# An attention and two feed-forward blocks on one core: more subtractions and the landmark sums issued to GpSimd

## The chip, the core and the metric

The kernel runs on one core of one Trainium2 chip. A core has five engines with a queue of instructions each, which they work off in order: TensorE (PE; its weight loads are PEld), VectorE (DVE), ScalarE (ACT), GpSimd (POOL) and SyncE (SP), which here issues every DMA. The metric is device time in microseconds (us), the median of three runs.

## The reference, cut to what matters

```python
def _attn_ref(q, k, v):                       # 4 batches, 8 heads, 576 positions, 64 wide
    q_lm = q.reshape(B, H, 32, S // 32, D).mean(axis=3)   # 32 landmarks: means of 18 positions
    k_lm = k.reshape(B, H, 32, S // 32, D).mean(axis=3)
    A, Bm, C = sm(q, k_lm), sm(q_lm, k_lm), sm(q_lm, k)   # three softmaxes
    Z = Bm.T / (norm_1(Bm) * norm_inf(Bm) + 1e-06)        # then 6 times: Z = 2 Z - Z Bm Z
    return A @ Z @ C @ v

def reference(...):
    x = attention as 2304 tokens x 512
    h = x @ w_in;   y = (h * cos(h)) @ w_out              # 512 -> 2048 -> 512
    h2 = y @ w_in2; return prelu(h2, alpha) @ w_out2      # 512 -> 2048 -> 512
```

All data are float32. q and k are drawn eight times as large as v.

## The kernel before, in words

**Split numbers.** A product of float32 matrices is made of three TensorE products. Each operand is held as a high half (a rounding copy, made by ScalarE) and a low half (the operand minus the high half, made by a subtraction). The subtractions all go through the helper `sub` at L323, so in the profile they are `L323 TENSOR_TENSOR`, on VectorE (DVE) or on GpSimd (POOL). `split` makes both halves of a tile 512 or 576 wide; `hl` does it for the second block's weights, `y_load` for its input (256 wide), and `tick` and `btick` for the activations (288 and 512 wide).

**First stage, some 535 us.** Attention runs in units of two batches and two heads: four units at the start (`unit`, m = 0) and four more later (m = 1), each group followed by the iteration for Z (`z_path`). `vprime` folds attention's last factor into the first weight matrix. The first block then runs as 128 ticks (`tick`): one tick is a product of 6 matmuls into a PSUM bank `h` (L986), the chain ACT L991, DVE L993, ACT L995 and L996, DVE L997 that makes h cos(h), its high half (ACT L1000), its low half (L323, 288 wide), and 12 matmuls of the second product (L1013). There are two banks `h`; L997 is the last reader of a bank, so L986 of the tick after next waits for it. The second four units, and `convert`, which turns the 64 pieces of weights from 64-bit to 32-bit numbers in three VectorE instructions (L474, L476, L478) with a DMA ahead and often one behind, run between the ticks.

**Landmark sums.** A landmark is a sum over 18 positions. Nine of these lie along the free axis of a tile, and that part is one VectorE reduction over 1152 elements: L609 for six of the eight sums of the first units, L645 for the eight of the second units. The other two of the first units go through nine matmuls each (L620), a copy and a transpose.

**Second stage, some 380 us.** The second block takes 512 tokens at a time; one `btick` is seven products of 256 columns (L1257, one level of Strassen's scheme), their combination on VectorE (L1280), the activation (L1321, L1324), its halves (L1326, L323) and 24 matmuls of 512 columns (L1338). A last piece of 256 tokens uses L1302.

**What sets the order.** The class `Plan` takes every operation with its dependencies, a duration for each engine that may do it, and a due time, and lays them out engine by engine on a model of time; what it puts out is the fixed order of each engine's queue. Where an operation may go to two engines, it is given to the one that ends it first by that model, after a bias is taken off: 0.2 us for POOL and for ACT (`PB`, `AB`). The tiles share memory areas with a fixed number of buffers per name (three of `cf`, which `convert` uses, three of `raw`). An operation can be placed once the buffer it needs has been given up. In the profile, and in the rows of order below, nearly all SBUF tiles read `m`; `h`, `x` and `acc` are PSUM banks.

## Time and profile before

| | before |
|---|---|
| time, median of three runs | 916.64 us |
| lowest of the runs | 913.74 us |
| the profiled execution, its own time | 916.43 us |
| its span, from first to last instruction | 914.6 us |
| TensorE busy, granted clock (mean) | 835.4 us, 0.958 |
| VectorE busy | 680.6 us |
| ScalarE busy | 501.1 us |
| GpSimd busy | 181.8 us |

Busy time is a sum over the whole span. The two stages have different limits, so the shares have to be read stage by stage. The granted clock is a share of 2.4 GHz. A row's duration on VectorE or GpSimd runs from start to end of the instruction and includes any time in which it stands still.

### The profile page before, as it was taken

The numbers are of one execution on the slowest core, as the hardware profiler recorded it, in microseconds if no ns is written. First come the engines' busy times: TensorE is split into PE (matmuls) and PEld (weight loads), VectorE is DVE, ScalarE is ACT, GpSimd is POOL, SyncE is SP. The second block draws the span as 40 slices with busy tenths as digits, with TensorE's granted clock in tenths as the row PEclk, the third lists the DMA queues.
The fourth block names the chain that finished last, engine by engine and source line by source line (L and its number), as shares of the span: only waits on it lengthen the run. The fifth ranks groups of instructions, "written<-read, shape, count | busy, mean of one in ns | idle before, by whom it ended". The sixth has DMA issues, their size and how long they took to land.

```text
span 914.6 us, 15709 instructions
## 1 busy us (share of the span) xinstructions
PE 835.4 (91%) x5674; PEld 749.3 (82%) x5674; DVE 680.6 (74%) x1316; ACT 501.1 (55%) x1165; POOL 181.8 (20%) x182
## 2 busy tenths in 40 slices
PE   5885889896999899999898989999999999999997
PEld 4563778684888889899888978999999899998896
DVE  6889978889898677988998686875566556556663
ACT  4754769687667576575766843353344234433431
POOL 2022231212113011312542222310021012000100
PEclk8895899797999999999999999999999999999999
DMA  9978699978769899798557421113013111310140
GB/s 229 238 225 238 193 239 206 229 166 246 207 191 286 271 310 304 232 309 303 165 184 239 135 84 47 47 58 82 24 47 99 52 35 57 83 35 25 48 126 23
DMA packets 98013, 144.42 MB, mean 158 GB/s; under 512 B 28560, under 2 KB 63888, under 8 KB 97936
## 3 DMA queue, kind: packets, MB, share of 16 engines
q1 hardware_dynamic: 97936, 143.43, 54.0%
q8 instruction: 44, 0.72, 0.3%
q14 instruction: 33, 0.27, 0.1%
HBM read 96.35 MB, written 38.67 MB: 148 GB/s over the span
## 4 chain that ended last, share of the span: by engine, by line
PE 54%; DVE 20%; DMA 15%; ACT 5%; issue 4%; SPq 1%; POOL 0%; DVEq 0%; ACTq 0%; POOLq 0%
PE acc L1338 21%; PE h L1257 9%; PE x L1257 7%; PE acc L1013 6%; DMA m<-in_moe_w_out_dram 3%; PE h L986 3%; DVE m L323 3%; DMA m<-w1d 2%; DVE m L476 2%; DVE m L478 2%; DVE m L997 2%; DVE m L993 2%; DMA y1d<-m 1%; DMA m<-in_moe_w_in_dram 1%; DVE m L474 1%
## 5 line engine op out<-in xcount | busy, mean ns | idle before, releaser
L323 POOL TENSOR_TENSOR m<-m,m 128x288 fp32r<-128x288 f32 (+4 forms) x149 | 151.2, 1021 | 559.3 <-ACT m L1000 201.6
L1013 PE MATMUL acc<-m,m 128*128 128x288 f32 x1536 | 239.5, 304 | 3.3 <-DVE m L1033 2.4
L1013 PEld LDWEIGHTS acc<-m,m 128*128 128x128 f32 x1536 | 219.9, 194 | 8.9 <-issue 4.4
L1338 PE MATMUL acc<-m,m 128*128 128x512 f32 x864 | 208.4, 393 | 0.8 <-DVE m L323 0.4
L323 DVE TENSOR_TENSOR m<-m,m 128x512 fp32r<-128x512 f32 (+4 forms) x283 | 177.3, 648 | 41.5 <-ACT m L458 16.6
L1338 PEld LDWEIGHTS acc<-m,m 128*128 128x128 f32 x864 | 159.4, 189 | 32.4 <-DVE m L323 0.9
L986 PE MATMUL h<-m,m 128*128 128x288 f32 x768 | 132.5, 310 | 30.9 <-DVE m L997 25.1
L986 PEld LDWEIGHTS h<-m,m 128*128 128x128 f32 x768 | 113.0, 196 | 41.5 <-DVE m L997 32.9
L1257 PE MATMUL h<-m,m 128*128 128x256 f32 x768 | 106.3, 281 | 0.4 <-ACT m L318 0.4
L1326 ACT ACTIVATE m<-m 128x512 fp32r<-128x512 f32 (+1 forms) x80 | 46.3, 588 | 109.0 <-DVE m L1324 106.5
L1257 PEld LDWEIGHTS h<-m,m 128*128 128x128 f32 x768 | 99.2, 188 | 2.9 <-ACT m L318 0.6
L1280 DVE TENSOR_TENSOR m<-h,m 128x512 f32<-128x512 f32 x32 | 22.1, 690 | 81.9 <-ACT m L318 81.9
L1257 PE MATMUL x<-m,m 128*128 128x256 f32 x576 | 80.3, 283 | 1.8 <-ACT m L318 1.8
L1000 ACT ACTIVATE m<-m 128x288 fp32r<-128x288 f32 x128 | 55.9, 443 | 43.0 <-DVE m L997 40.8
L318 ACT ACTIVATE m<-h 128x256 f32<-128x256 f32 (+3 forms) x105 | 42.2, 404 | 64.3 <-PE h L1257 58.7
L1257 PEld LDWEIGHTS x<-m,m 128*128 128x128 f32 x576 | 73.0, 188 | 3.6 <-ACT m L318 2.0
L995 ACT ACTIVATE m<-m 128x288 f32<-128x288 f32 x128 | 56.0, 443 | 30.7 <-DVE m L993 30.2
L1117 ACT ACTIVATE m<-m 128x512 fp32r<-128x512 f32 x68 | 41.4, 628 | 43.7 <-PE h L1257 20.0
L997 DVE SCALAR_TENSOR_TENSOR m<-m,h 128x288 f32<-128x288 f32 x128 | 56.3, 446 | 10.1 <-ACT m L996 9.6
L993 DVE SCALAR_TENSOR_TENSOR m<-h,m 128x288 f32<-128x288 f32 x128 | 57.1, 448 | 8.2 <-ACT m L991 7.7
L991 ACT ACTIVATE m<-h 128x288 int32<-128x288 f32 x128 | 51.6, 403 | 20.4 <-PE h L986 19.9
L458 ACT ACTIVATE m<-m 128x512 fp32r<-128x512 f32 (+1 forms) x72 | 45.2, 631 | 28.3 <-DMA m<-w1d 18.5
(156 smaller groups left out, 949.6 us busy)
## 6 DMA issues: line engine op xcount, KB each, us to landing
m<-in_moe_w_out_dram SPq DMA_DIRECT2D x32, 512.0 KB, 5.2
m<-in_moe_w_in_dram SPq DMA_DIRECT2D x32, 512.0 KB, 5.6
m<-wi2d SPq DMA_DIRECT2D x56, 256.0 KB, 3.2
y1d<-m SPq DMA_DIRECT2D x40, 288.0 KB, 4.8
m<-w1d SPq DMA_DIRECT2D x32, 256.0 KB, 4.8
m<-m SPq DMA_DIRECT2D x32, 256.0 KB, 4.5
vvd<-m SPq DMA_DIRECT2D x32, 256.0 KB, 4.6
m<-vvd SPq DMA_DIRECT2D x16, 512.0 KB, 6.0
```

The source lines that it names most:

```text
L323: ENG[e].tensor_tensor(o, a, b, op=ALU.subtract)
L458: op(act(n), lambda e: nc.scalar.activation(hi.t[:, 0:n], sl(f.t), AF.Copy), r=[f], w=[hi, lo], target=target, after=after)
L986: nc.tensor.matmul(out=hp.t[:, 0:CW], lhsT=w_[:, js], rhs=x[:, cs], start=(i == 0), stop=(i == 5))
L991: op(act(CW, True), lambda e: nc.scalar.activation(k_.t, hp.t[:, 0:CW], AF.Copy, scale=INV2PI), r=[hp], w=[k_], target=T + 0.8)
L993: op(dve(CW), lambda e: nc.vector.scalar_tensor_tensor(u.t, hp.t[:, 0:CW], INV2PI, k_.t, op0=ALU.mult, op1=ALU.subtract), r=[hp, k_], w=[u])
L995: op(act(CW), lambda e: nc.scalar.activation(u.t, u.t, AF.Sin, scale=math.pi), rw=[u], aset="sin")
L997: op(dve(CW), lambda e: nc.vector.scalar_tensor_tensor(hc.t, u.t, 1.0, hp.t[:, 0:CW], op0=ALU.subtract, op1=ALU.mult, reverse0=True), r=[h ...
L1000: op(act(CW), lambda e: nc.scalar.activation(gh.t, hc.t, AF.Copy), r=[hc], w=[gh, gl])
L1013: nc.tensor.matmul(out=yg[o].t[:, 0:CW], lhsT=w_.t[:, sl], rhs=x.t, start=(j == ja and i == 0), stop=(j == jb and i == 2),)
L1257: nc.tensor.matmul(out=rv(k), lhsT=a_.t[:, p, c2, js], rhs=b_.t[:, q_, c2, 0:hw], start=(first and c2 == 0 and i == 0), stop=(c2 == 1 and ...
L1326: op(act(w), lambda e, m_=m_, gh=gh: nc.scalar.activation(gh.t[:, 0:w], m_.t[:, 0:w], AF.Copy), r=[m_], w=[gh, gl])
L1338: nc.tensor.matmul(out=ya[n][t].t, lhsT=gv(x_), rhs=r_.t, start=(st and k == 0), stop=(en and k == 2))
```

## The change

The plan's cost of an elementwise operation on GpSimd goes from n/480 + 0.15 us to n/440 + 0.3 us, and a new bias `SB` = 1.6 us takes the place of `PB` = 0.2 us for POOL, so that an operation that may go to VectorE or GpSimd goes to GpSimd unless it would end there over 1.6 us later by the model. The landmark sums of the first units may go to VectorE (one reduction, as before) or to GpSimd, where they are four additions of halves and a copy; the form with matmuls (L620) is gone. Those of the second units go to GpSimd always, as five additions, with a buffer of `cf` for the partial sums.

```diff
-KN = dict(..., PB=0.2, AB=0.2, ..., LM=126, ..., QN=2, KA=0.004, ...)
+KN = dict(..., PB=0.2, AB=0.2, ..., QN=2, SB=1.6, KA=0.004, ...)
+        def bias(o, x):
+            return KN["SB"] if x == "POOL" else BIAS.get(x, 0.0)
-                        max(free[x], o.est, sl) + dx - BIAS.get(x, 0.0) < s + d - BIAS.get(e, 0.0)
+                        max(free[x], o.est, sl) + dx - bias(o, x) < s + d - bias(o, e)
     def pool(n):
-        return ("POOL", n / 480.0 + 0.15)
+        return ("POOL", n / 440.0 + 0.3)
@@ landmark sums, first units (a: 128 x 1152)
-                    op(dve(1152), lambda e, a=a, ls=ls: nc.vector.tensor_reduce(...))       # L609
-                    ... or nine matmuls, a copy and a transpose                             # L620
+                    x = a.t.rearrange("p (h r d) -> p h r d", h=2, d=D)
+                    y = ls.t.rearrange("p (h r d) -> p h r d", h=2, d=D)
+                    add(y, x[:, :, 0:4], x[:, :, 4:8])
+                    add(y[:, :, 0:2], y[:, :, 0:2], y[:, :, 2:4])
+                    add(y[:, :, 0:1], y[:, :, 0:1], y[:, :, 1:2])
+                    z = ls.t[:, P:2 * P].rearrange("p (h d) -> p h d", h=2)
+                    add(z, y[:, :, 0], x[:, :, 8])
+                    nc.gpsimd.tensor_copy(ls.t[:, 0:P], ls.t[:, P:2 * P])
+                op([("POOL", 3.9), ("DVE", 2.1)], lm, r=[a], w=[ls])
@@ landmark sums, second units (t: 128 x 1152)
-                op(dve(1152), lambda e, t=t, lt=lt: nc.vector.tensor_reduce(...))           # L645
+                tr_ = sb("cf", [P, 4 * P])
+                    add(y, x[:, 0:4 * P], x[:, 4 * P:8 * P])
+                    add(y[:, 0:2 * P], y[:, 0:2 * P], y[:, 2 * P:4 * P])
+                    add(y[:, 0:P], y[:, 0:P], y[:, P:2 * P])
+                    add(y[:, 0:P], y[:, 0:P], x[:, 8 * P:9 * P])
+                    add(lt.t, z[:, :, 0], z[:, :, 1])
+                op(("POOL", 1088 / 440.0 + 1.2), tree, r=[t], w=[lt, tr_])
```

Since the plan orders everything anew, the queues differ in many places. Three of them follow. Lines of the changed kernel stand 3 to 14 higher: its L326 is L323 before, L477, L479 and L481 are L474, L476 and L478, L1007 and L1011 are L993 and L997, L614 is L609.

First, GpSimd at its start, after the tables of constants. Before:

```order
L323 TENSOR_TENSOR m_125<-m_110,m_124 128x512
L323 TENSOR_TENSOR m_178<-m_131,m_177 128x512
L323 TENSOR_TENSOR m_367<-m_110,m_366 128x512
L323 TENSOR_TENSOR m_537<-m_492,m_537 128x512
L323 TENSOR_TENSOR m_598<-m_540,m_598 128x512
```

and in the changed kernel:

```order
L326 TENSOR_TENSOR m_165<-m_111,m_164 128x512
L620 TENSOR_TENSOR m_71<-m_90 128x512
L620 TENSOR_TENSOR m_71<-m_71 128x2x128
L620 TENSOR_TENSOR m_71<-m_71 128x2x64
L620 TENSOR_TENSOR m_71<-m_71,m_90 128x128
L629 COPY m_71<-m_71 128x128
L326 TENSOR_TENSOR m_197<-m_145,m_196 128x512
L326 TENSOR_TENSOR m_225<-m_181,m_224 128x512
```

The first of three landmark sums of the first units stands between two weight subtractions; the other five stay on VectorE.

Second, VectorE around the 102nd to 104th tick, where L474, L476 and L478 convert weights and L323 makes low halves. Before:

```order
L993 SCALAR_TENSOR_TENSOR m_837<-h,m_837 128x288
L997 SCALAR_TENSOR_TENSOR m_837<-m_837,h 128x288
L323 TENSOR_TENSOR m_699<-m_4677,m_699 128x512
L323 TENSOR_TENSOR m_878<-m_837,m_878 128x288
L997 SCALAR_TENSOR_TENSOR m_837<-m_837,h 128x288
L474 TENSOR_SCALAR m_131<-m_93 128x512
L993 SCALAR_TENSOR_TENSOR m_837<-h,m_837 128x288
L323 TENSOR_TENSOR m_878<-m_837,m_878 128x288
L476 SCALAR_TENSOR_TENSOR m_131<-m_93,m_131 128x512
L474 TENSOR_SCALAR m_192<-m_93 128x512
L997 SCALAR_TENSOR_TENSOR m_837<-m_837,h 128x288
```

and in the changed kernel:

```order
L1007 SCALAR_TENSOR_TENSOR m_836<-h,m_836 128x288
L477 TENSOR_SCALAR m_181<-m_93 128x512
L326 TENSOR_TENSOR m_726<-m_4699,m_726 128x512
L1011 SCALAR_TENSOR_TENSOR m_836<-m_836,h 128x288
L1007 SCALAR_TENSOR_TENSOR m_836<-h,m_836 128x288
L479 SCALAR_TENSOR_TENSOR m_181<-m_93,m_181 128x512
L477 TENSOR_SCALAR m_111<-m_93 128x512
L481 SCALAR_TENSOR_TENSOR m_181<-m_93,m_181 128x512
L1011 SCALAR_TENSOR_TENSOR m_836<-m_836,h 128x288
```

The 288-wide subtractions of the ticks have left this stretch of VectorE's queue; the conversions stay.

Third, GpSimd among the ticks of the second four units in the changed kernel (before, this stretch of its queue holds only L323 and L752):

```order
L326 TENSOR_TENSOR m_879<-m_836,m_879 128x288
L652 TENSOR_TENSOR m_145<-m_71 128x512
L652 TENSOR_TENSOR m_145<-m_145 128x256
L652 TENSOR_TENSOR m_145<-m_145 128x128
L652 TENSOR_TENSOR m_145<-m_145,m_71 128x128
L652 TENSOR_TENSOR m_71<-m_145 128x64
L326 TENSOR_TENSOR m_879<-m_836,m_879 128x288 x6
L652 TENSOR_TENSOR m_181<-m_71 128x512
```

A landmark sum is now five rows between the ticks' subtractions, and `m_145` and `m_181` are two of the three `cf` buffers that the conversions also use.

Counted over the order, these instructions stand on each engine. The first stage's VectorE counts are those ahead of its first L1280 (L1294).

| | DVE before | DVE after | POOL before | POOL after |
|---|---|---|---|---|
| low halves, 288 wide (ticks) | 56 | 15 | 72 | 113 |
| low halves, 512 wide, first stage | 47 | 14 | 24 | 57 |
| 576 wide (L323), first stage | 8 | 3 | 8 | 13 |
| 576 wide (L752) | 4 | 2 | 4 | 6 |
| 256 wide, first stage | 11 | 6 | 11 | 16 |
| landmark sums, first units | 6 | 5 | 0 | 3 |
| landmark sums, second units | 8 | 0 | 0 | 8 |
| low halves, 512 wide, second stage | 117 | 57 | 8 | 68 |

## Rows read from the trace of the kernel before

**Rows 1.** The page: busy time, then the chain that ended last, by engine

```profile
span 914.6 us, 15709 instructions
...
PE 835.4 (91%) x5674; PEld 749.3 (82%) x5674; DVE 680.6 (74%) x1316; ACT 501.1 (55%) x1165; POOL 181.8 (20%) x182
...
PE 54%; DVE 20%; DMA 15%; ACT 5%; issue 4%; SPq 1%; POOL 0%; DVEq 0%; ACTq 0%; POOLq 0%
```

**Rows 2.** Windows by stage: us, busy (xcount) by engine, PEclk, DMA share, GB/s

```profile
0.00:89.00 89.00, 60.52 (x477) 42.90 (x478) 72.44 (x163) 46.09 (x106) 17.12 (x22) 0.83 0.87 232
89.00:297.00 208.00, 181.62 (x1331) 159.03 (x1331) 180.37 (x382) 150.90 (x348) 51.45 (x49) 0.92 0.84 218
297.00:520.00 223.00, 206.78 (x1447) 198.35 (x1446) 184.79 (x359) 151.79 (x384) 62.47 (x61) 0.98 0.77 252
...
535.00:860.00 325.00, 321.98 (x2000) 290.09 (x1999) 207.50 (x347) 127.02 (x278) 43.35 (x44) 0.99 0.18 55
```

**Rows 3.** Chain of waits, 535 to 914.6, by line: share of that stretch

```profile
by line: PE acc L1338 49.5%; PE h L1257 21.2%; PE x L1257 15.9%; PE h L1302 3.0%; PE x L1302 3.0%; DVE m L323 1.6%; DMA m<-wi2d 1.4%; ACT m L1117 0.6%; DVE m L1145 0.5%; POOL m L1145 0.5%; DVE m L1324 0.4%; ACT m L318 0.4%; DVE m L1280 0.3%
```

**Rows 4.** Waits, 0 to 535: waiter, releaser, total us, times, longest us

```profile
PEld h L986 <- DVE m L997: 32.9, 30, 6.1
...
SPq L501 <- DVE m L478: 48.2, 21, 4.9
```

**Rows 5.** VectorE by line and shape, 0 to 530: xcount | busy us, mean ns

```profile
L478 DVE SCALAR_TENSOR_TENSOR m<-m,m 128x512 int32<-128x512 int32 x64 | 52.5, 821 | 0.2
L476 DVE SCALAR_TENSOR_TENSOR m<-m,m 128x512 int32<-128x512 int32 x64 | 48.6, 760 | 0.2
L474 DVE TENSOR_SCALAR m<-m 128x512 int32<-128x512 int32 x64 | 37.7, 594 | 21.9 <-DMA m<-in_moe_w_out_dram 14.3 <-DMA m<-in_moe_w_in_dram 4.6 <-DMA wi2d<-m 2.1
L323 DVE TENSOR_TENSOR m<-m,m 128x512 fp32r<-128x512 f32 x47 | 34.4, 733 | 15.8 <-ACT m L458 15.6
L323 DVE TENSOR_TENSOR m<-m,m 128x288 fp32r<-128x288 f32 x56 | 32.2, 578 | 2.2 <-ACT m L1000 1.2
...
L645 DVE TENSOR_REDUCE m<-m 128x64 f32<-128x1152 f32 x8 | 17.9, 2235 | 2.0 <-ACT m L318 1.8 <-ACT m L655 0.2
L609 DVE TENSOR_REDUCE m<-m 128x128 f32<-128x1152 f32 x6 | 12.7, 2118 | 0.7 <-DMA m<-in_q_dram 0.7
```

**Rows 6.** GpSimd by line and shape, 0 to 530, same columns

```profile
L323 POOL TENSOR_TENSOR m<-m,m 128x288 fp32r<-128x288 f32 x72 | 67.4, 938 | 228.8 <-ACT m L1000 201.6 <-PE acc L1013 15.9 <-PE x L597 9.5
L323 POOL TENSOR_TENSOR m<-m,m 128x512 fp32r<-128x512 f32 x24 | 32.1, 1338 | 112.4 <-ACT m L458 111.9 <-ACT m L1117 0.3
...
L323 POOL TENSOR_TENSOR m<-m,m 128x576 fp32r<-128x576 f32 x3 | 4.5, 1491 | 7.8 <-ACT m L458 7.8
```

**Rows 7.** Timeline from 357.4: start us, us, engine, line, operation

```profile
357.45 0.68 DVE L476 SCALAR_TENSOR_TENSOR m<-m,m 128x512 int32<-128x512 int32 x1
...
357.72 1.08 POOL L323 TENSOR_TENSOR m<-m,m 128x288 fp32r<-128x288 f32 x1 [4.92 <-ACT m L1000]
...
358.05 0.45 DVE L993 SCALAR_TENSOR_TENSOR m<-h,m 128x288 f32<-128x288 f32 x1
...
358.42 0.93 DVE L478 SCALAR_TENSOR_TENSOR m<-m,m 128x512 int32<-128x512 int32 x1
```

**Rows 8.** Timeline, VectorE, from 379.9 on

```profile
380.89 0.41 DVE L474 TENSOR_SCALAR m<-m 128x512 int32<-128x512 int32 x1
```

**Rows 9.** TensorE, the landmark sums by matmul, 0 to 530, columns as rows 5

```profile
L620 PE MATMUL h<-m,m 128*64 128x128 f32 x36 | 6.3, 349 | 5.9 <-DMA m<-in_k_dram 5.9
```

**Rows 10.** Timeline of the second product, around 617 to 624

```profile
617.68 0.69 DVE L323 TENSOR_TENSOR m<-m,m 128x512 fp32r<-128x512 f32 x1 [0.31 <-ACT m L1326]
...
620.12 2.00 DVE L323 TENSOR_TENSOR m<-m,m 128x512 fp32r<-128x512 f32 x3
...
621.50 0.86 PE L1338 MATMUL acc<-m,m 128*128 128x512 f32 x3
...
628.40 1.58 PE L1257 MATMUL h<-m,m 128*128 128x256 f32 x12
```

More of the change, by code (lines that the diff above doesn't have):

```diff
@@ L616, in unit @@
-                pl = bank(0)
-                def lm(e, a=a, pl=pl):
-                    for r in range(NR):
-                        nc.tensor.matmul(
-                            out=pl.t[0:64, 0:P], lhsT=poolm,
-                            rhs=a.t.rearrange("p (h r d) -> p r h d", h=2, d=D)[:, r],
-                            start=(r == 0), stop=(r == NR - 1), skip_group_check=True,
-                        )
-                op(pe(NR * P, 4), lm, r=[a], w=[pl])
-                ls = atb(0, "ls", [P, P])
@@ L627, in unit, with lm, add @@
-                op([act(128), dve(128)], lambda e, ls=ls, pl=pl: copy(e, ls.t[0:64], pl.t[0:64, 0:P]),
-                   r=[pl], w=[ls])
-                op(pe(128, 2), lambda e, i=i, ls=ls: nc.tensor.transpose(
-                    pt.t[:, i * P:i * P + 64], ls.t[0:64], ident[0:64, 0:64]), r=[ls], w=[pt])
+                ls = atb(0, "ls", [P, 4 * P])
+                def lm(e, a=a, ls=ls):
+                    if e == "DVE":
+                        nc.vector.tensor_reduce(
+                            ls.t[:, 0:P].rearrange("p (h d) -> p h d", h=2),
+                            a.t.rearrange("p (h r d) -> p h d r", h=2, d=D), axis=AX.X, op=ALU.add)
+                        return
+                    def add(o, x, y):
+                        nc.gpsimd.tensor_tensor(o, x, y, op=ALU.add)
+                    x = a.t.rearrange("p (h r d) -> p h r d", h=2, d=D)
[6 more added lines that the diff above has]
+                    nc.gpsimd.tensor_copy(ls.t[:, 0:P], ls.t[:, P:2 * P])
@@ L631, in unit @@
+                op([("POOL", 3.9), ("DVE", 2.1)], lm, r=[a], w=[ls])
+                op(("PE", 0.16), lambda e, i=i, ls=ls: nc.tensor.matmul(
+                    out=pt.t[:, i * P:i * P + 64], lhsT=ls.t[:, 0:P], rhs=poolm, start=True, stop=True,
+                    skip_group_check=True), r=[ls], w=[pt])
             for hh in range(2):
@@ L744, in unit @@
             mxa, sma = atb(m, "amx", [P, NBK, 1]), atb(m, "asm", [P, NBK, 1])
-            tt = [("POOL", 1.11), dve(S)]
+            tt = [pool(S), dve(S)]
             op(dve(S), lambda e, mxa=mxa, at=at: nc.vector.reduce_max(mxa.t, at.t, axis=AX.X), r=[at], w=[mxa])
```

21 lines of the change are left out of this document (7 added, 14 removed).

## The prediction

> **What bounds the kernel now.** I read the windows by stage first [rows 2]. From 535 us on TensorE is busy for 321.98 of 325 us at a granted clock of 0.99, and the chain of waits there is nearly all matmuls: VectorE's lines add up to 1.6 + 0.5 + 0.4 + 0.3 = 2.8% [rows 3]. The second stage is bound by TensorE; an engine that is freed there gives nothing back. Up to 520 us no engine fills the time: TensorE is busy for 60.5 + 181.6 + 206.8 = 449 us, VectorE for 72.4 + 180.4 + 184.8 = 438 us (84%), GpSimd for 17.1 + 51.5 + 62.5 = 131 us, and the DMA engines for 0.77 to 0.87 of it [rows 2]. Here the page's chain decides [rows 1]: VectorE holds 20% of 914.6, 183 us. Taking off 2.8% of the last 380 us (11 us) leaves 172 of the first 535 us, a share of 0.32. The waits name the place [rows 4]: TensorE's weight loads for a tick's first product waited 32.9 us, 30 times, for L997, which frees the PSUM bank, and the DMA queue 48.2 us for L478. GpSimd holds 0% of the chain [rows 1]. So VectorE in the first stage is where the change can act.
>
> **What is removed from VectorE.** By the counts of the order in the first stage: 41 subtractions 288 wide at 0.578 us make 23.7 us, 33 of 512 at 0.733 make 24.2, five of 576 and two of L752 priced at the 512 row 5.1, five of 256 priced at the 288 row 2.9, eight L645 17.9 and one L609 2.1 [rows 5]. That is 76 us; a sum that comes to VectorE (L1145) and some small copies take back about 2, so 74 us.
>
> **What is added to GpSimd.** 41 at 0.938 us make 38.5, 33 at 1.338 make 44.2, seven 576 wide at 1.491 make 10.4 [rows 6]. The trace has no addition on GpSimd narrower than 256 and none of the new ones, so I bound them: the two rows for 288 and 512 differ by 0.400 us over 224 elements, 1.79 ns each, which gives 0.88 us for 256, 0.65 for 128 and 0.54 for 64. Five more 256 wide are 4.4 us, and one landmark sum is 1.34 + 0.88 + 2 x 0.65 + 0.54 = 4.1 us; were its three narrow steps as long as a 288 row, it would be 5.0. I take 4.1, since the additions are of the same kind as those rows; eleven make 45 us. In all 143 us come to GpSimd's 131: some 274 of 520 us. It has room, but each sum is later than VectorE's 2.235 us was [rows 5].
>
> **What the two engines do to each other.** This is the price that decides. In [rows 7] L476 runs its 0.68 us while a subtraction on GpSimd starts and takes 1.08 us. L993, which starts during the latter and reads one operand from PSUM, takes 0.45 us. L478, which reads two from SBUF and starts 0.38 us before GpSimd ends, takes 0.93 and ends 0.55 us after it, where L476 of the same shape took 0.68. L474 takes 0.41 us alone [rows 8], but 0.594 on the mean, L476 0.760 and L478 0.821 [rows 5]. So the three conversion lines, which all stay on VectorE, stand still for 64 x (0.821 - 0.68 + 0.760 - 0.68 + 0.594 - 0.41) = 26 us beside GpSimd's 131 us: 0.20 us per us of GpSimd. The Trainium skill agrees (SBUF — State Buffer, section "Who interferes with whom"): a VectorE instruction with two SBUF inputs contends with a GpSimd one that reads SBUF, the first to start holds the shared port, and one with at most one SBUF input outside the two-port modes does not contend.
>
> For the 143 us that come I take the same rate: 28 us more standing still, and about 3 us more on the subtractions that stay: alone, instructions of their widths take the 0.45 and 0.68 us of L993 and L476 [rows 7], so 15 x (0.578 - 0.45) + 14 x (0.733 - 0.68) = 2.7 us stand still at GpSimd's present time, and its time about doubles. Its ends: nothing, if the new GpSimd work falls beside L993, L997 and other PSUM readers; and one us for one us, 143, if every instruction meets a conversion. I take the rate measured, since the mixture of lines that stays is the same.
>
> **The sum.** 74 - 31 = 43 us less of VectorE. Not all of it is on the path: I let each us count by the share of the first stage in which the chain is on VectorE, 0.32, so 14 us. The ends give 74 x 0.32 = 24 us gained, and (143 - 74) x 0.32 = 22 us lost. Against the profiled execution, 916.43 us (914.6 of it span), this makes 902.4; I forecast 903 us. That execution lies 0.2 us under the median of 916.64, so nothing is added for it.
>
> **What costs nothing.** The matmuls of L620 that go are 6.3 us of TensorE [rows 9], in the first 89 us, where TensorE is busy for 60.5 [rows 2] and so has time for them; the gain of at most 6.3 us that they may bring I leave to the range. In the second stage 60 subtractions of 512 move. Their cover is the order: VectorE ended a low half at 618.4 (617.68 + 0.69), and the next group of L1338 starts only at 621.50; weight halves were made from 620.12 to 622.12, and the next products start at 628.40 [rows 10]. On GpSimd two low halves take 2.7 us in place of 1.4, three weight halves 4.0 in place of 2.0. This fits in 3 and 6 us. If the cover were gone, one us for each of 32 pieces of 512 tokens would be 32 us; I find no row that says so.
>
> **The rivals.** *The queue on VectorE empties faster than in proportion* (0.26): L997 is late because conversions stand ahead of it in the queue, so the 32.9 us that TensorE waits for it [rows 4] could shrink to little. All of it gone gives 916.4 - 33 = 883; I put the case at 880 to 895. For it: these are 30 waits, the longest 6.1 us, spread over the stage. Against it: from 297 to 520 us TensorE is already busy for 206.8 of 223 us, and the DMA engines for 0.77 to 0.87 [rows 2].
>
> *A new wait eats the gain* (0.16): a landmark sum is needed before its unit's scores, and on GpSimd it stands in one queue with the ticks' low halves, which wait for ScalarE. Eleven sums that are 4.1 - 2.2 = 1.9 us later are 21 us; if most of it lay on the chain, 910 to 922 is left. The sums of the second units also hold a buffer of `cf`, three of which feed the conversions, and through L478 the DMA queue. Against it: the second units run beside ticks, and TensorE has other work.
>
> *The shared port costs more than the offload saves* (0.15): this is the case on the other side. Its place is the stretch from 297 to 520 us, where conversions alternate with ticks and nearly each tick now has a GpSimd subtraction. It decides when the added standing still is over 74 us, that is 0.52 us per added us of GpSimd, against 0.20 measured. Working against me is that GpSimd is then busy for half of the time, so that conversions meet it more often one after another. At one for one 22 us are lost: 938; with GpSimd's own delays I put it at 922 to 950. The Trainium skill has this rule (Perfetto Trace Analysis, section "Optimizing Scalar/DVE Operations"): as the two engines share a read port, moving operations between them might not help. By the trace it holds for the conversions and not for L993.
>
> That the change does not do what it says is no case: the order shows the moves.
>
> **How the numbers follow.** The forecast, a gain of a part of VectorE's relief, has 0.43 and by itself 895 to 910; the rivals have 0.26, 0.16 and 0.15. A change of 2%, about what a measurement of this kernel tells from none, lies at 898.3 and 935. Faster by more are the first rival and a fifth of the forecast's interval: 0.26 + 0.10 = 0.36. Slower by more is half of the last rival: 0.08. Within 2%: 0.56. Cutting a tenth off the lower end (within 880 to 895) leaves 886, a twentieth or so off the upper (within 922 to 950) 931. The range holds both signs because the price of the port does.
>
> **What would show it.** In the changed profile VectorE should be busy for some 395 us up to the start of the second stage, GpSimd for some 270, with L477, L479 and L481 longer than L474, L476 and L478 are now: together 2.6 us where they are 2.175. The wait of the ticks' first product for L1011 should fall below 32.9 us, the second stage should keep its 380 us, and a landmark sum on GpSimd should take some 4 us. I am wrong if the conversions' mean grows by over a us for the three, if TensorE waits for L631, L671 or for POOL's L326, or if the last 380 us get longer.

## The result, and the profile after

The changed kernel takes 920.66 us (median) where the kernel before takes 916.25 on the same chip: a ratio of 1.0062, 95% interval 1.0038 to 1.0086. It is slower by 0.6%, where a gain of 14 us was forecast. One of the eleven runs of the kernel before, at 1329.78 us, is left out of the ratio, which is an estimate by itself and not the quotient of the two medians (1.0048).

The page of the changed kernel: span, busy time, and the chain that ended last by engine.

```profile
span 918.9 us, 15839 instructions
...
PE 829.3 (90%) x5640; PEld 740.8 (81%) x5640; DVE 630.1 (69%) x1138; ACT 497.8 (54%) x1155; POOL 422.9 (46%) x414
...
PE 51%; DVE 22%; DMA 15%; issue 5%; ACT 4%; SPq 3%; POOL 0%; DVEq 0%; ACTq 0%
```

VectorE lost 50 us of busy time against [rows 1], GpSimd's more than doubled, and VectorE's share of the chain rose from 20 to 22%. The windows by stage, with the columns of [rows 2]:

```profile
0.00:89.00 89.00, 58.44 (x452) 40.45 (x454) 79.52 (x166) 48.89 (x109) 37.51 (x43) 0.83 0.87 245
89.00:297.00 208.00, 177.94 (x1308) 153.88 (x1305) 161.90 (x351) 147.68 (x343) 104.43 (x111) 0.95 0.81 216
297.00:520.00 223.00, 202.93 (x1443) 194.71 (x1442) 162.37 (x298) 150.36 (x378) 115.68 (x114) 0.99 0.76 247
535.00:860.00 325.00, 321.14 (x1997) 289.26 (x1997) 200.98 (x278) 123.94 (x273) 132.27 (x115) 0.99 0.19 55
```

Up to 520 us VectorE is busy for 403.8 us (437.6 before), GpSimd for 257.6 (131.0). So the work did move, but the wait it was to shorten [rows 4] did not get shorter. Waits of the changed kernel up to 535 us (waiter, releaser, total us, times, longest us):

```profile
PEld h L1000 <- DVE m L1011: 36.6, 40, 2.4
DVE m L1011 <- ACT m L1010: 28.0, 28, 2.6
...
SPq L504 <- DVE m L481: 56.4, 21, 11.4
```

TensorE's weight loads wait 36.6 us for VectorE where they waited 32.9, the DMA queue 56.4 where it was 48.2. VectorE by line and shape in the changed kernel, columns as in [rows 5]:

```profile
L479 DVE SCALAR_TENSOR_TENSOR m<-m,m 128x512 int32<-128x512 int32 x64 | 58.3, 911 | 0.5
...
L1011 DVE SCALAR_TENSOR_TENSOR m<-m,h 128x288 f32<-128x288 f32 x128 | 57.0, 447 | 37.9 <-ACT m L1010 28.0 <-POOL m L326 9.3
L481 DVE SCALAR_TENSOR_TENSOR m<-m,m 128x512 int32<-128x512 int32 x64 | 54.1, 846 | 0.3
L477 DVE TENSOR_SCALAR m<-m 128x512 int32<-128x512 int32 x64 | 42.5, 667 | 7.4 <-DMA wi2d<-m 3.5 <-DMA m<-in_moe_w_in_dram 3.2 <-DMA m<-in_moe_w_out_dram 0.6
...
L326 DVE TENSOR_TENSOR m<-m,m 128x512 fp32r<-128x512 f32 x14 | 13.7, 975 | 3.3 <-ACT m L461 2.8 <-PE acc L1027 0.4
L326 DVE TENSOR_TENSOR m<-m,m 128x288 fp32r<-128x288 f32 x15 | 13.4, 901 | 5.2 <-ACT m L1014 5.2
```

The costliest lines with SBUF operands only grew: the three conversions to 911, 846 and 667 ns, the subtractions left on VectorE to 975 and 901 (733 and 578 before). L1011, which reads PSUM, did not (447 ns, 446 before). It waits 28.0 us for ScalarE's L1010, where L997 waited 9.6 us for L996: a part of the time that VectorE was freed of is spent on that.

Where the two profiled executions part is seen at the start of the 65th tick's L993 (L1007 after), first in the kernel before, then in the changed one (timeline: start us, us):

```profile
346.45 0.46 DVE L993 SCALAR_TENSOR_TENSOR m<-h,m 128x288 f32<-128x288 f32 x1
```

```profile
351.26 0.46 DVE L1007 SCALAR_TENSOR_TENSOR m<-h,m 128x288 f32<-128x288 f32 x1 [0.56 <-ACT m L1005]
```

Up to there 4.8 us are lost. From there to the first combination of the second stage (528.9 and 531.2 us) 2.5 us are gained, and the second stage is 1.9 us longer (385.7 and 387.6 us): 4.2 us together. Single executions differ by as much: in the one profiled of short_sums (below), the kernel before with less work, that tick starts at 351.4 us. So where the 0.6% are lost is not shown by this.

### The profile page after: what moved, and what is told of

It reads as the page before. It is cut to its first block, busy times and chain, and to the rows that moved or that the text cites. A ratio compares the mean times of both kernels' runs of the same rounds, so it can differ in the third digit from the quotient of the medians.

```text
span 918.9 us, 15839 instructions
## 1 busy us (share of the span) xinstructions
PE 829.3 (90%) x5640; PEld 740.8 (81%) x5640; DVE 630.1 (69%) x1138; ACT 497.8 (54%) x1155; POOL 422.9 (46%) x414
## 4 chain that ended last, share of the span: by engine, by line
PE 51%; DVE 22%; DMA 15%; issue 5%; ACT 4%; SPq 3%; POOL 0%; DVEq 0%; ACTq 0%
PE acc L1352 20%; PE h L1271 9%; PE x L1271 7%; PE acc L1027 7%; PE h L1000 3%; DVE m L481 3%; DMA m<-w1d 3%; DVE m L326 3%; DVE m L479 2%; DMA m<-in_moe_w_in_dram 2%; DMA wi2d<-m 2%; DMA m<-y1d 2%; DVE m L1011 2%; DVE m L477 2%; DVE m L1007 2%
## 5 line engine op out<-in xcount | busy, mean ns | idle before, releaser
L326 POOL TENSOR_TENSOR m<-m,m 128x512 fp32r<-128x512 f32 (+4 forms) x318 | 344.6, 1096 | 433.4 <-ACT m L1340 147.4
L1027 PE MATMUL acc<-m,m 128*128 128x288 f32 x1536 | 232.3, 298 | 10.1 <-DVE m L1047 9.4
L1027 PEld LDWEIGHTS acc<-m,m 128*128 128x128 f32 x1536 | 213.2, 189 | 15.9 <-ACT m L1010 4.5
L1352 PEld LDWEIGHTS acc<-m,m 128*128 128x128 f32 x864 | 159.7, 190 | 30.9
L1000 PEld LDWEIGHTS h<-m,m 128*128 128x128 f32 x768 | 112.4, 196 | 43.2 <-DVE m L1011 36.6
L326 DVE TENSOR_TENSOR m<-m,m 128x512 fp32r<-128x512 f32 (+3 forms) x114 | 114.7, 1024 | 36.1 <-ACT m L1340 15.4
L1011 DVE SCALAR_TENSOR_TENSOR m<-m,h 128x288 f32<-128x288 f32 x128 | 57.0, 447 | 37.9 <-ACT m L1010 28.0
L1294 DVE TENSOR_TENSOR m<-h,m 128x512 f32<-128x512 f32 x32 | 22.1, 691 | 86.2 <-ACT m L321 83.0
L321 ACT ACTIVATE m<-h 128x256 f32<-128x256 f32 (+2 forms) x103 | 41.7, 407 | 65.1 <-PE h L1271 61.2
L1007 DVE SCALAR_TENSOR_TENSOR m<-h,m 128x288 f32<-128x288 f32 x128 | 57.5, 450 | 20.2 <-ACT m L1005 19.7
L1009 ACT ACTIVATE m<-m 128x288 f32<-128x288 f32 x128 | 56.4, 442 | 24.6 <-DVE m L1007 24.0
L1271 PE MATMUL x<-m,m 128*128 128x256 f32 x384 | 57.6, 284 | 2.5 <-ACT m L321 2.2
L479 DVE SCALAR_TENSOR_TENSOR m<-m,m 128x512 int32<-128x512 int32 x64 | 58.3, 911 | 0.5
L1271 PE MATMUL h<-m,m 128*128 128x256 f32 x384 | 56.4, 282 | 1.3 <-ACT m L321 1.3
L1010 ACT ACTIVATE m<-m 128x288 f32<-128x288 f32 x128 | 56.1, 440 | 2.3
```

The costliest lines, as they stand in the source:

```text
L326: ENG[e].tensor_tensor(o, a, b, op=ALU.subtract)
L479: op(dve(512), lambda e: nc.vector.scalar_tensor_tensor(cf.t, rv(1), -0x40000000, cf.t, op0=ALU.bitwise_and, op1=ALU.bitwise_or), r=[raw], ...
L1000: nc.tensor.matmul(out=hp.t[:, 0:CW], lhsT=w_[:, js], rhs=x[:, cs], start=(i == 0), stop=(i == 5))
L1007: op(dve(CW), lambda e: nc.vector.scalar_tensor_tensor(u.t, hp.t[:, 0:CW], INV2PI, k_.t, op0=ALU.mult, op1=ALU.subtract), r=[hp, k_], w=[u])
L1009: op(act(CW), lambda e: nc.scalar.activation(u.t, u.t, AF.Sin, scale=math.pi), rw=[u], aset="sin")
L1010: op(act(CW), lambda e: nc.scalar.activation(u.t, u.t, AF.Square, scale=math.sqrt(2.0)), rw=[u])
```

## The experiments

Two theories stood against each other at first. *Port*: GpSimd's reads make VectorE stand still, and that eats the relief. *Path*: VectorE's relief doesn't count, since something else sets the pace. Two came later: *order*, that the new plan's order is itself slower, and *lateness*, that TensorE waits for low halves which GpSimd makes later. Ratios are to the kernel before, timed in the same round of runs; its medians there were 914.3 to 917.2 us. The diffs are shortened (`...`). "Narrow" stands for 16 columns, in a buffer that has been written in full once.

### Relief of VectorE, with and without work for GpSimd

**relief_alone**: the order of before, VectorE's subtractions cut short, GpSimd as before.

```diff
     def sub(e, o, a, b):
+        ...
+        if e == "DVE" and len(o.shape) == 2 and key in wide:   # written in full once
+            o, a, b = o[:, 0:16], a[:, 0:16], b[:, 0:16]
+        ...
         ENG[e].tensor_tensor(o, a, b, op=ALU.subtract)
```

> The kernel before, its order and its engines unchanged, but each VectorE low-half subtraction of a two-dimensional tile computes only its first 16 columns once its buffer has been written in full one time (the rest of the low half keeps old values). This takes some 50 of VectorE's 438 us in the first 520 us away and puts nothing on GpSimd. Theory PATH (VectorE's load in the first stage is off the path; the stage ends when the second attention, the V' products at the DMA's pace and the remaining ticks are through): within 5 us of before, 911 to 917 us. Theory PORT (relief is worth a third of itself, and the shared port took it back in the changed kernel): 16 us or more faster, 900 us or less.

Measured: 906.39 us, 0.9897 (0.984 to 0.9955). That lies between the two theories. VectorE has 30 us less to do up to the last tick (406.6 for 436.4), and relieving it for nothing is worth 9.4 us; 1 to 3 us of that lie in the second stage (382.6 us long; 383.9 to 385.9 in the traces of the four kernels that leave it as it was before).

**subs_in_place**: the same order; three of four of VectorE's subtractions in the first stage are issued to GpSimd.

```diff
+        if stage[0] == 1 and e == "DVE":
+            turn[0] += 1
+            if turn[0] % 4:
+                e = "POOL"
...
         ENG[e].tensor_tensor(o, a, b, op=ALU.subtract)
```

> The order of the kernel before, with three of four of the subtractions that the helper has on VectorE in the first stage put on GpSimd at their places (about as many as the change moves); the landmark sums and the second stage as before. Nothing is left out. It is the offload without the new order. If the new order is what costs (all_on_vector 1.017 against before_on_vector 1.0025), and the offload itself gains what the prediction worked out, 902 to 911 us. If moving subtractions to GpSimd gives as much as it takes (subs_only 0.999, order_on_vector against the changed kernel 1.3 us), 912 to 920 us. If it takes more, above 921.

Measured: 919.25 us, 1.0037 (1.0005 to 1.0069): no gain, a small loss. The two windows up to the last tick, relief_alone first (its last stretch, 344 to 510), then subs_in_place (349 to 524):

```profile
344.00:510.00 166.00, 157.06 (x1147) 152.48 (x1145) 138.21 (x283) 116.99 (x301) 54.19 (x54) 1.00 0.77 251
```

```profile
349.00:524.00 175.00, 159.21 (x1136) 152.87 (x1135) 135.00 (x241) 116.48 (x299) 94.62 (x95) 0.99 0.73 236
```

VectorE has as little to do in the one as in the other, 138 and 135 us, and the stretch takes 166 and 175 us. GpSimd's 54 and 95 us differ, and so does when the low halves come: TensorE's weight loads wait for GpSimd's here, 14.2 us in all,

```profile
PEld acc L1019 <- POOL m L329: 7.9, 11, 2.4
PEld x L917 <- POOL m L329: 6.3, 8, 1.3
```

where they wait 1.3 us in relief_alone and 4.3 in the changed kernel. So the 13 us between these two kernels (1.0037 less 0.9897) are not the price of GpSimd's reads alone; lateness is in them.

**short_sums**: the kernel before with the eight reductions of L645 over a ninth of their elements.

```diff
-    lt.t, t.t.rearrange(...).rearrange("p r (x t) -> p x t r", t=2),
+    lt.t, t.t.rearrange(...).rearrange("p r (x t) -> p x t r", t=2)[:, :, :, 0:1],
```

> The kernel before with the eight reductions of L645 over 128 elements in place of 1152; the landmarks of the second units are so means of two positions. VectorE is relieved of some 15 us of long instructions with nothing put on GpSimd and the order unchanged. If this work counts by the prediction's share of 0.32, 5 us: 908 to 912. If long reductions stand in the way of the ticks beyond their length (sums_on_vector was 8.6 us slower than the changed kernel), 903 to 908. If the stretch up to 346 us is paced by the loads of w1d (narrow_v_loads) and VectorE's relief doesn't count there, 913 to 917.

Measured: 915.98 us, 0.9987 (0.9953 to 1.0022). VectorE has 16 us less to do up to the last tick (420.0 for 436.4) and the time stays; the interval leaves room for 4 us at the most. All of these reductions lie between 143 and 208 us.

**narrow_v_loads**: the kernel before, with 28 of the 32 loads of `w1d` for `vprime` 64 columns wide.

```diff
-    nc.sync.dma_start(out=f.t[:, 0:512], in_=w1d[p, :, fb * 512:fb * 512 + 512])
+    nc.sync.dma_start(out=f.t[:, 0:n], in_=w1d[p, :, fb * 512:fb * 512 + n])   # 64, once loaded in full
```

> The kernel before, but each load of the first weight matrix for a V' product (256 KB) brings only its first 64 columns once its buffer has been loaded in full one time (the other columns are old values). Order and engines are unchanged; 6.3 of 123 MB of the first stage's DMA go. PATH: up to the 65th tick the stage waits for such transfers, so that tick starts 10 us or more before 346 us, and the time falls to 895 to 908. If VectorE bounds that part: no change, 914 to 918.

Measured: 904.59 us, 0.9895 (0.9843 to 0.9947), with VectorE as busy as before (435.1 us). The 65th tick starts at 338 us for 346; from there the two take 566 and 568 us. So these loads help to pace the part ahead of 346 us, where the sums lie.

### What GpSimd's reads cost

**no_port**: the changed kernel, GpSimd's two-dimensional subtractions narrow.

```diff
+        ...
+        if e == "POOL" and len(o.shape) == 2 and key in wide:
+            o, a, b = o[:, 0:16], a[:, 0:16], b[:, 0:16]
```

> The changed kernel, order and engines unchanged, but each GpSimd low-half subtraction of a two-dimensional tile computes only its first 16 columns once its buffer has been written in full one time. GpSimd's 423 us fall to some 150, so VectorE's conversions hardly stand still and low halves are ready early. PORT: 15 us or more faster than the changed kernel, 905 us or less. PATH: within 6 us of the changed kernel, 914 to 921. Theory SUMS (the late landmark sums on GpSimd cost the gain): a few us faster, because the sums no longer stand behind long subtractions, 908 to 916.

Measured: 907.47 us, 0.9895 (0.9863 to 0.9928). That is between the bounds of the theories. It takes away the reads, but GpSimd's lateness too.

**no_lock** and **before_nolock**: about as late and as long, but nearly without the reads, in the changed kernel and in the kernel before.

```diff
+        if e == "POOL" and len(o.shape) == 2:
+            n = o.shape[1]
+            ENG[e].tensor_tensor(o[:, 0:16], a[:, 0:16], b[:, 0:16], op=ALU.subtract)
+            w = f32(o) if o.dtype == F32R else o
+            nc.gpsimd.memset(w[:, 16:n], 0.0)
+            nc.gpsimd.memset(w[:, 16:min(n, int(1.56 * n) - 254)], 0.0)
+            return
```

> The changed kernel, order and engines unchanged, but each GpSimd low-half subtraction of a two-dimensional tile reads only 16 columns and then fills the rest of the low half with zeros by two writes without a read, sized so that the three together take about as long (0.8 us for 288, 1.3 us for 512; the low halves' values are left out). GpSimd is as busy and its results as late, but its reads beside VectorE are nearly gone. The run with 16 columns alone came out at 907.5 us against 920.7. PORT: the standing still beside reads was the cost, so 905 to 911 us, and L478's counterpart falls to about 0.7 us on the mean. LATE (low halves that are ready late, or the queue on GpSimd, are the cost): 917 to 923, as the changed kernel.

> The kernel before, with GpSimd's two-dimensional subtractions of L323 in the form of no_lock: 16 columns are subtracted, the rest of the duration is write-only memsets, so these low halves are zeros beyond 16 columns. If GpSimd's reads are paid by VectorE in proportion (port), the kernel before pays for its 131 us of them about half of what the changed kernel pays for 268 (22 us): 903 to 909 us. If only the changed kernel's order makes the reads dear, 914 to 918 us, no change.

Measured: no_lock 898.22 us, 0.9851 (0.9786 to 0.9916); before_nolock 895.7 us, 0.9801 (0.9772 to 0.983). Both are faster than their expectations had it. In the changed kernel late low halves are not the cost, since they are about as late here (TensorE waits 3.2 us for them, 4.3 in the changed kernel). The expectation for the kernel before was half of the changed kernel's price, and it is about the same: 18 us there, 19 in the changed kernel (1.0062 less 0.9851; the interval of no_lock is 6 us to either side). Without the reads the change would still not gain. What bounds both is seen in the stretch from the 65th to the last tick (columns as in [rows 2]); the kernel before, the changed one, before_nolock, no_lock:

```profile
346.00:518.00 172.00, 160.23 (x1141) 155.03 (x1141) 149.92 (x282) 117.23 (x300) 56.34 (x54) 0.98 0.74 241
```

```profile
351.00:520.00 169.00, 158.32 (x1150) 153.43 (x1149) 134.32 (x239) 117.35 (x298) 91.23 (x91) 1.00 0.72 237
```

```profile
345.00:502.00 157.00, 153.53 (x1144) 151.65 (x1143) 131.97 (x283) 118.08 (x300) 53.92 (x156) 1.00 0.81 265
```

```profile
345.00:502.00 157.00, 153.92 (x1143) 151.68 (x1143) 113.45 (x237) 116.76 (x296) 82.40 (x266) 1.00 0.77 254
```

Without the reads TensorE is busy for 98% of 157 us, whether VectorE works for 132 or for 113 us. With them TensorE stands idle for 12 us before and 11 after, and is also busy for 7 and 4 us longer.

**zeros_locked**: the control, since the low halves of no_lock are zeros. The changed kernel with `b = a` in the same place.

> The changed kernel, but each two-dimensional subtraction of L326 on GpSimd subtracts its first operand from itself: both reads of SBUF and the duration stay, the low halves become zeros (so the outputs lose those low halves), as they were in no_lock. It is the control of no_lock. If the reads cost the time (port), this takes the changed kernel's time, 917 to 924 us. If the zeros made no_lock fast (a weight load or a product with zeros, or a rounding copy), it takes 895 to 905 us.

Measured: 914.12 us, 1.0005 (0.9979 to 1.0032). The zeros are not the main part of what made no_lock fast; yet this is 5 us less than the changed kernel. It can't be told whether the zeros, shorter subtractions or an earlier start give that: with one tile as both operands GpSimd took 757 ns for 288 columns, where it took 888, and it no longer waited for ScalarE's high half (116.2 us of its idle time in the changed kernel), but for VectorE's L1011 (123.8 us). So the reads cost the changed kernel between 14 us (1.0005 less 0.9851) and 19. The kernel before has no such control.

### In which stage

**nolock_first** and **nolock_second**: the edit of no_lock ahead of the second stage only, and in it only (a flag set by the first combination, L1294).

> The changed kernel with GpSimd's two-dimensional subtractions in the write-only form of no_lock up to the start of the second stage, and as in the changed kernel behind it. The low halves of the first stage's GpSimd subtractions are zeros beyond 16 columns. no_lock took 22 us off in all, zeros_locked (same zeros, reads kept) 5 us off. If the first stage pays for the reads, this keeps most of it: 898 to 906 us, with the second stage some 387 us long as in the changed kernel. If the second stage pays, 914 to 920 us.

> The complement: write-only subtractions on GpSimd from the start of the second stage on only, whose low halves there are zeros beyond 16 columns; the first stage as in the changed kernel. If the second stage, which the prediction called free, pays for the reads of the 60 subtractions that moved there, it gets 4 to 7 us shorter (387.7 us in the changed kernel, 381.4 in no_lock): 912 to 917 us. If it is bound by TensorE alone, no change: 918 to 924 us.

Measured: 906.54 us, 0.9892 (0.9859 to 0.9925), and 915.5 us, 1.0004 (0.9969 to 1.0038). By the ratios the first stage pays 15.6 us of the reads and the second 5.3, together 20.9 (19 in no_lock), each with some 4 us to either side and with the zeros in it. The first expectation was just missed. The traces agree for the second stage: it takes 381.3 us in nolock_second and in no_lock, and 385.9 to 387.6 in the three kernels that have it as the changed kernel does (itself, nolock_first and sums_on_vector below). In before_nolock it takes 381.8 for 383.9 to 385.9: the kernel before paid a part of this already. In the same 325 us of the second stage TensorE is busy for longer without the reads than its 321.14 above; windows of nolock_second:

```profile
535.00:860.00 325.00, 324.32 (x2039) 293.30 (x2039) 165.97 (x287) 128.10 (x280) 125.83 (x340) 1.00 0.19 55
```

**second_on_vector**: the changed kernel, with the second stage's subtractions back on VectorE.

```diff
+        if stage[0] == 2 and e == "POOL":
+            e = "DVE"
```

> The changed kernel with the second stage's subtractions of GpSimd put back on VectorE, at their places; the first stage as in the changed kernel. Nothing is left out. If GpSimd's reads and lateness cost the second stage something and VectorE has room there, 914 to 918 us, the second stage 383 to 386 us long. If the second stage is bound by TensorE whatever these engines do, as the prediction has it, 918 to 924 us. Above 925 us VectorE had no room there.

Measured: 918.89 us, 1.0043 (1.0015 to 1.007); the stage is 383.0 us long in its profile. The difference of 1.7 us to the changed kernel points the same way, but the intervals overlap. The traces are clearer: with its subtractions on VectorE the stage takes 383.0 to 383.3 us in three kernels of the new order (this one, order_on_vector and all_on_vector below), 3 us less than in the three that have them on GpSimd.

### The parts of the change, and the order

**subs_only** and **sums_only**: the kernel before with the new bias and cost alone; the changed kernel with the old ones. **late_sums**: before, with only the second units' sums on GpSimd.

> The kernel before with the new bias of 1.6 us and the new cost of GpSimd, landmark sums as before. SUMS: faster than the changed kernel by 5 us or more, 905 to 915. PATH: 914 to 922, as both kernels. PORT: like the changed kernel or slower, 917 to 925, as most of GpSimd's new time is subtractions.

> The changed kernel's landmark sums on GpSimd, with the bias for GpSimd (0.2 us) and its cost as before. SUMS: slower than before by 3 us or more, 919 to 925. PATH: within 3 us of before. PORT: a gain of some 5 us, since the sums take 20 us off VectorE and bring little standing still: 909 to 913.

> The kernel before with one part of the change alone: the eight landmark sums of the second units as five additions on GpSimd, with the bias and the cost of an operation on GpSimd as before, and the first units' sums as before. Nothing is left out. If these sums help because they take 18 us of VectorE's reductions away (sums_on_vector was 8.6 us slower than the changed kernel), 906 to 913 us. If GpSimd's reads cost what VectorE saves (port), 914 to 920 us. Above 922 the new order, not the sums, is what costs.

Measured: subs_only 915.94 us, 0.9991 (0.9964 to 1.0017); sums_only 931.17, 1.0163 (1.0112 to 1.0214); late_sums 917.54, 1.0047 (1.0024 to 1.007). No part gains. In sums_only the loss is at the start: its first tick comes at 104.5 us for 89.4, since seven of the eight early sums then are VectorE's and the route by matmuls is gone. Each of these kernels has an order of its own, so they mix the part with its order.

**sums_on_vector**, **order_on_vector**, **all_on_vector**: the changed kernel's order, with the sums, the subtractions, or both issued to VectorE at the same places. **before_on_vector**: the order of before, all subtractions on VectorE.

```diff
     def sub(e, o, a, b):
-        ENG[e].tensor_tensor(o, a, b, op=ALU.subtract)
+        ENG["DVE"].tensor_tensor(o, a, b, op=ALU.subtract)    # order_, all_, before_on_vector
...
+        nc.vector.tensor_reduce(lt.t, ..., axis=AX.XY, op=ALU.add); return   # sums_, all_on_vector
         add(y, x[:, 0:4 * P], x[:, 4 * P:8 * P])               # not reached
...                                                             # first units likewise
```

> The changed kernel, order unchanged, but every landmark sum that GpSimd has in it runs as one VectorE reduction at the same place of the order (the cf buffer stays held). SUMS: the tick that is the 65th starts 5 us or more earlier than the changed kernel's 351 us and the time is 911 to 917. PATH: what the first 350 us wait for is neither engine, so the time is within 3 us of the changed kernel, 918 to 924.

> The changed kernel, order of everything unchanged, but every low-half subtraction by the helper runs on VectorE; the landmark sums stay on GpSimd. It tells the new order from the new engine. If the new order alone is the better one (theory ORDER: GpSimd spoils it): 910 to 916, below the changed kernel. PORT with a relief that is nearly worthless: 916 to 924, as VectorE gets 110 us back in the first stage and loses most of its standing still. RELIEF WORTH A FIFTH (the run with narrow subtractions gained 10 us for some 50): 925 to 940.

> The kernel before in its own order, but every subtraction of the helper at L323 runs on VectorE at the place in the program where GpSimd would have got it. Nothing is left out. If moving these subtractions gives as much as it takes (port), 913 to 921 us. If the offload that the kernel before already has is worth its relief of VectorE, 925 us or more. It differs from order_on_vector in its order alone, so the difference of the two is that of the orders with no subtraction on GpSimd.

> The changed kernel's order with both its parts undone: every subtraction of the helper and every landmark sum runs on VectorE, at the places that the changed kernel's order gives them. Nothing is left out. Against before_on_vector (the order of before, the same work on the same engine, ratio 1.0025) this is the price of the new order alone. If the order costs nothing, 915 to 921 us; if the changed kernel's order is what costs, and the offload hides a part of it, 925 to 940 us.

Measured: sums_on_vector 929.23 us, 1.0146 (1.006 to 1.0231); order_on_vector 921.67, 1.0076 (1.0041 to 1.0111); before_on_vector 916.22, 1.0025 (0.9995 to 1.0054); all_on_vector 929.5, 1.0173 (1.0113 to 1.0232). sums_on_vector is slower than either theory had it. Three things follow. In either order the kernel takes the same time with the subtractions on VectorE and on GpSimd: 921.67 against 920.66 in the new one; 1.0025, 1.0000 and 1.0037 in the old one with none, some and most of them on GpSimd. In the old order this is no wonder: up to the last tick VectorE is busy for 445.5 us with all of them, only 9 more than before, since its conversions take 422, 685 and 708 ns there (594, 760 and 821 before). In the new order, order_on_vector and second_on_vector differ in the first stage's subtractions alone; VectorE is busy for 438.0 and 402.9 us, and these 35 us bring 3 us (1.0076 less 1.0043, with 4 to either side). Windows of order_on_vector:

```profile
0.00:90.00 90.00, 56.04 (x438) 39.37 (x438) 74.67 (x171) 45.38 (x102) 17.74 (x29) 0.82 0.83 224
90.00:358.00 268.00, 227.90 (x1619) 199.90 (x1620) 218.66 (x511) 184.32 (x429) 31.84 (x43) 0.94 0.83 231
358.00:526.00 168.00, 157.78 (x1149) 152.98 (x1149) 144.65 (x326) 117.41 (x296) 2.91 (x2) 1.00 0.72 238
```

In its own order the change is worth 10 us (1.0173 less 1.0062), nearly all of it by the sums (1.0173 less 1.0076 with the subtractions on VectorE; with them on GpSimd 1.0146 less 1.0062, whose intervals touch). And with all of them on VectorE the new order is 13.5 us slower than the old one. That is no clean price of the order: the new plan had laid those places out for GpSimd, and without the matmuls of L620 VectorE has two sums more. None of the kernels that leave nothing out is faster than the kernel before by more than its interval.

## Why the prediction was wrong

The kernels side by side. VectorE and GpSimd: busy up to the last tick's L993, by the windows of each trace; the wait is that of TensorE's weight loads for a tick's first product, as in [rows 4].

| | ratio | VectorE | GpSimd | wait |
|---|---|---|---|---|
| before | 1 | 436.4 | 131.1 | 32.9 |
| changed | 1.0062 | 403.8 | 257.6 | 36.6 |
| subs_in_place | 1.0037 | 403.3 | 220.8 | 33.5 |
| relief_alone | 0.9897 | 406.6 | 128.3 | 31.0 |
| before_nolock | 0.9801 | 406.5 | 126.0, writes | 20.7 |
| no_lock | 0.9851 | 359.9 | 240.1, writes | 22.1 |
| zeros_locked | 1.0005 | 387.3 | 222.8, reads one tile | 29.7 |
| before_on_vector | 1.0025 | 445.5 | 12.3 | 30.5 |
| order_on_vector | 1.0076 | 438.0 | 52.5 | 32.3 |
| second_on_vector | 1.0043 | 402.9 | 258.9 | 38.6 |

Rows of the waits on which the last column rests; relief_alone, subs_in_place, before_nolock, no_lock and zeros_locked in turn:

```profile
PEld h L992 <- DVE m L1003: 31.0, 30, 5.1
```

```profile
PEld h L992 <- DVE m L1003: 33.5, 30, 6.1
```

```profile
PEld h L993 <- DVE m L1004: 20.7, 17, 4.5
```

```profile
PEld h L1007 <- DVE m L1018: 22.1, 22, 2.9
```

```profile
PEld h L1002 <- DVE m L1013: 29.7, 32, 2.6
```

Four of the first five kernels have 403 to 407 us of VectorE, and their ratios run from 0.980 to 1.006. **The sum of VectorE's busy time is not what sets the time of the first stage.** By the prediction's steps:

- *What bounds the kernel.* Half right. The place was right: TensorE waits for L997. The reason, that VectorE has too much to do, was not. Relief shortens that wait little (32.9 to 31.0 in relief_alone), and 47 us less of VectorE between before_nolock and no_lock, which differ in order too, don't shorten it (20.7 and 22.1). Taking GpSimd's reads away alone takes 12 and 15 us off it; in the changed kernel at least 8 of these are the reads', since with them and with zeros it is 29.7.
- *Removed from VectorE, added to GpSimd.* Right by the counts. GpSimd is busy for 257.6 us (some 270 forecast). The eight sums of the second units take 3.6 to 4.4 us each for 4.1. But the relief was priced by durations, and a row's end overlaps the start of the next (in the timeline below L1007 ends at 389.61 us and L479 starts at 389.53). Added up to the first combination, VectorE's durations fell by 46 us, as forecast (43); its busy time fell by 36.
- *The rate of standing still.* Right as a rate, not in its parts. The conversions grew by 64 x 0.249 = 16 us, the subtractions that stayed by 15 x 0.323 + 14 x 0.242 = 8. That is 24 us for 127 us more of GpSimd, 0.19 per us for 0.20; of the 31 us forecast for 143, 28 were the conversions' and 3 the subtractions'. The conversions' means add up to 2.42 us; 2.6 was forecast. VectorE came out at 403.8 us for some 395.
- *Each us counts 0.32.* **This is the step that failed.** It gave every us of VectorE's busy time one weight, whichever work it was and whether work or standing still. In the new order the first stage's subtractions take 35 us off VectorE when they go to GpSimd, standing still already taken off, and bring 3 us (second_on_vector against order_on_vector, 4 to either side); the step gives 11.

  The other runs show weights from nothing to 0.5. In the order of before, relief_alone and before_nolock both take 30 us off VectorE. Taken from its own subtractions, these bring some 7 us in the first stage, 0.2 for each. Taken from its standing still, by removing GpSimd's reads, they bring some 14 to 16 (18 less the 2 to 4 by which the second stage is shorter), 0.5 for each. The 16 us of sums in short_sums brought nothing, nor did the 47 us between before_nolock and no_lock, which differ in order and where TensorE binds.

  The sum had 74 x 0.32 = 24 us gained and 31 x 0.32 = 10 us lost. By an estimate with the weights of the order of before it has (74 - 18) x 0.2 = 11 us gained, the second units' sums counting nothing, and 24 x 0.5 = 12 us lost: no gain. That standing still weighs more than work is not fully shown: before_nolock has no control for its zeros, and with 5 us less for them, as in zeros_locked, the two weights could not be told apart. Why it should weigh more, because it comes when ScalarE has just ended a tick's high half, with the next tick's L997 in VectorE's queue, is argued from the timeline below.
- *A share of the chain as a weight.* It also hides where relief can count at all. Ahead of 346 us the sums' relief did not (short_sums; the loads of `w1d` matter there). Behind it TensorE was idle for 12 us in all. That is a guide to what can be gained in that stretch and no bound: before_nolock gained 15 us there, since TensorE's busy time fell too, from 160.23 to 153.53 us (granted clock 0.98 and 1.00).
- *The second stage costs nothing.* Wrong, by little. It got 1.9 us longer in the two profiles, and by all traces takes 385.9 to 387.6 us for 383.9 to 385.9. GpSimd's reads cost 5.3 us in it (nolock_second). The low halves had cover, since with them as late it takes 381.3 us; what was left out is that VectorE stands still there too: in the 325 us it is busy for 200.98 us with the reads and for 165.97 without.
- *The rivals.* The queue that empties faster fell: the wait grew. The measured time lies in the interval given for a new wait (910 to 922 us), and so in the whole range, but that is luck: the late sums fell as a cause in this order, since on VectorE they are 8.6 us worse. The shared port was the right mechanism in the old order, where it leaves 9 us of relief, but not by the bound given for it: 0.52 us of standing still per added us was asked for and 0.19 measured. At that rate it could take the gain only because a us of VectorE's work counted for so little. Two of the prediction's own signs of being wrong came in, both small: TensorE waits 4.3 us for POOL's L326, and the second stage is longer.

Still open are two things. The reads cost the kernel before as much as the changed one, though it has half of them: 0.14 us for each us of GpSimd before, 0.05 to 0.07 after. So the estimate above rests on the order of before, and how the changed kernel's loss splits into relief, reads and order is not shown. That the price flattens once TensorE binds is an argument from the 157 us stretches and was not tried alone. And the price of the new order lies somewhere between 0 and 13 us; the prediction had no term for it.

## What to carry to other kernels

Before you move work from VectorE to GpSimd, look in the trace which VectorE instructions get longer beside GpSimd's reads, and what stands behind them in the queue. Don't give every us of a busy engine one weight: 35 us less of VectorE brought some 3 us here in one order, and 30 us less brought 9 us or 18 in the other. Judge the gain that is possible by the idle time of the engine that binds, stretch by stretch, and not by a share of the chain; and where a planner lays everything out anew, give the new order a term of its own, of either sign.

## What the runs showed of the hardware

How an instruction stands still is seen in the timeline of the changed kernel (start us, us):

```profile
389.17 0.44 DVE L1007 SCALAR_TENSOR_TENSOR m<-h,m 128x288 f32<-128x288 f32 x1
389.20 0.81 POOL L326 TENSOR_TENSOR m<-m,m 128x288 fp32r<-128x288 f32 x1 [1.20 <-ACT m L1014]
389.53 1.02 DVE L479 SCALAR_TENSOR_TENSOR m<-m,m 128x512 int32<-128x512 int32 x1
...
394.90 0.81 POOL L326 TENSOR_TENSOR m<-m,m 128x288 fp32r<-128x288 f32 x1 [2.19 <-ACT m L1014]
395.08 1.18 DVE L479 SCALAR_TENSOR_TENSOR m<-m,m 128x512 int32<-128x512 int32 x1
```

L479 starts during the subtraction on GpSimd and ends 0.54 us (389.53 + 1.02 less 390.01) and 0.55 us behind its end, whenever it started. L1007, which reads PSUM, takes its 0.44 us beside it. L477, which reads one tile, gets longer as well: 667 ns on the mean, where it takes 507 in no_lock and 433 in order_on_vector. In no_lock the same conversion beside memsets:

```profile
383.63 0.33 POOL L330 MEMSET m<- 128x272 f32 x1
383.80 0.68 DVE L486 SCALAR_TENSOR_TENSOR m<-m,m 128x512 int32<-128x512 int32 x1
...
384.02 0.25 POOL L331 MEMSET m<- 128x179 f32 x1
```

It takes 0.68 us, as L476 does in [rows 7]. This agrees with the Trainium skill (SBUF — State Buffer, section "Who interferes with whom"): a VectorE instruction with two SBUF inputs contends with GpSimd instructions that read SBUF, and not with those that only write.

A subtraction of 16 columns still takes VectorE 275 ns on the mean, with standing still in it (176 is the median), 0.48 of the 578 ns for 288 columns, so that cutting instructions short relieves it less than their widths say:

```profile
L329 DVE TENSOR_TENSOR m<-m,m 128x16 fp32r<-128x16 f32 x89 | 24.5, 275 | 27.3 <-ACT m L464 22.1 <-ACT m L1006 3.3 <-PE h L992 1.0
```

That is the row of relief_alone up to the second stage, by line and shape.
